# Attention and a two-layer network in one kernel: two copies put ahead of two weight sums, output transposes moved later

## The chip, the cores and the metric

The kernel runs on one core of a Trainium2 chip. Its time is the device time in microseconds (us), the median of three runs. The engines are TensorE (PE: matmuls; PEld: its weight loads, issued by the same sequencer), VectorE (DVE), ScalarE (ACT), GpSimd (POOL, which issues all loads here) and SyncE (SP, which issues all stores). Each engine works through its own list of instructions in order and waits for the others through semaphores.

## What is computed

Attention over 8 batches of 8 heads, 576 tokens each, head size 64, with 16 extra keys and values ("beacons") in front that every query sees; then a network of two layers without bias on the 4608 rows of 512 that the heads make together.

```python
k_all = np.concatenate([beacon_k, k], axis=2)
v_all = np.concatenate([beacon_v, v], axis=2)
scores = scale * np.matmul(q, k_all.transpose(0, 1, 3, 2))
causal[:, Nb:] = np.triu(np.ones((S, S), dtype=bool), k=1)
scores = np.where(causal, -1000000000.0, scores)
a = np.exp(scores - scores.max(-1, keepdims=True))
a /= a.sum(-1, keepdims=True) + 1e-09
attn = np.matmul(a, v_all)
...
x = attn.transpose(0, 2, 1, 3).reshape(B * S, H * D)
h = x @ w_in
g = np.maximum(0.01 * h, h)
return g @ w_out
```

## The kernel before

**The work's units.** Attention goes by pairs of heads: pair g = 0 to 31, four to a batch. For one pair:

- q and k are loaded by POOL (step N, load_natural), and turned on PE with the identity matrix into a PSUM tile "tp", which DVE copies to SBUF (step T, turn_natural, L177 to L184; T8.0 is q of pair 8, T8.1 its k).
- Scores are matmuls (L316) whose exponentials ACT writes (L331, L335); POOL sets the masked triangles to zero (L291). From pair 8 on this runs in "blocks" of three PSUM tiles over the pairs' columns in a row.
- Values (step v, value, L376): half 0 has 12 matmuls, half 1 has 18 (L361) into a PSUM tile "av" whose last column per row is the sum of the weights; DVE takes the reciprocal (L390) and multiplies (L391) into x_nat.
- The output's turn (x_transposes, L402 to L412): five transposes on PE (L407) from x_nat into a tile "tp", and one DVE copy into xT (L412). Here it is called x8 for pair 8, and so on.

The network goes by chunks of 512 tokens, nine in all. An "up" (moe1, L416) makes 128 hidden columns of a chunk: four matmuls of 512 columns (L427) into a PSUM tile, then the leaky ReLU on ACT into gT (L435). A "down" (moe2, L501) is eight matmuls of 256 columns (L509); the second layer is done as a 2 by 2 block product with seven products instead of eight, so it needs sums of weight blocks and of token blocks, which DVE makes: weight_sums (L447: part 0 at L453; part 1, two instructions of 128 x 2048 elements at L455 and L456; part 2 at L458) and token_sums (run at L784). Product 5 reads the result of part 0, product 6 that of L455, product 7 that of L456. Two downs share a PSUM tile, which ACT (L538, L574) or DVE (L535, L571) empties after the second.

**PSUM.** One pool, ps_one, has four banks; every tile named above but two of a block's three comes from it: tp, av, an up's and a down's acc, and the two halves of a block's first tile. When a tile is asked for, it takes a bank that an earlier tile has given up, and PE's first matmul into it waits until the engine that empties that bank is done.

**The order.** All five engines' lists are in the order in which the program states the steps (tc.manual_schedule, L906). Pairs 0 to 7 and the first chunk follow strings of steps written out by hand (L920 to L939; the letters are decoded at L863). Weight sums part 1, step t1, is in the last of them, L939, just ahead of the turns of pair 8. Then a list of events with due times takes over (L965 to L1009). The time unit is one pair; pair g's scores are due about g + 0.4. The due times of interest:

| step | due at | line |
|---|---|---|
| turn of q, k (T) of pair g | g - 1.15, g - 0.85 | L972, L973 |
| values half 0 of pair g | g + 2.25 (g + 2.05 for a batch's last pair) | L976, L977 |
| values half 1 | 0.37 later | L978 |
| output's turn, pairs 8 to 30 | 0.75 after half 0 | L980 |
| finish (a batch's last: its chunks may begin) | g + 3.5 | L985 |

The events are sorted by due time. Between two of them the loop at L997 to L1009 puts as many ups and downs as a straight line of progress asks for, some eight for one unit. The output's turn of the last pair (31) is not an event: it stands in the list for the last chunks (L1012). There, two chunks' first layer is also done with seven products (in_round).

Of the kernel before, what the change touches and what calls it, by code (L numbers as in the profile page):

```python
# [15 lines left out]
def kernel(  # L16
# [139 lines left out]
    def load_qk(g, which):  # L156
        b, hp, grp, rows = where(g)
        loaded["qk", g, which] = nc.gpsimd.dma_start(  # L158
            out=raw_of(b, grp)[which][rows],
            in_=(q, k)[which][b, 2 * hp : 2 * hp + 2].rearrange("h (p i) d -> p h i d", i=RI),  # L160
        )
# [5 lines left out]
    def load_natural(g, which):  # L167
        b, hp = divmod(g, NPAIR)
        t = natpool.tile([NR, S // NR, 2, D], BF16, name=("q_nat", "k_nat")[which])
        for par in range(2):  # L170
            nc.gpsimd.dma_start(  # L171
                out=t[:, :, par],
                in_=(q, k)[which][b, 2 * hp + par].rearrange("(t p) d -> p t d", p=NR),
            )
        nat.setdefault(g, []).append(t)

    def turn_natural(g, which):  # L177
        t = nat[g][which]
        ps = ps_one.tile([128, 1024], BF16, name="tp", tag="one")
        for n in range(S // NR):  # L180
            nc.tensor.transpose(  # L181
                ps[:, n * NR : (n + 1) * NR], t[:, n].rearrange("r h d -> r (h d)"), ident[0:NR, 0:NR]
            )
        nc.vector.tensor_copy(out=operand(g, which), in_=ps[:, 0:S])  # L184
# [22 lines left out]
    def load_v_cast(b, c):  # L207
        dst = v_bufs[b % 2]
        lo = 0
        if c == 0:  # L210
            nc.gpsimd.dma_start(
                out=dst[0:NB, 0, :, 0:D], in_=beacon_v[b].rearrange("h p d -> p h d")
            )
            lo = NB
        n = ROWS[c] - lo
        nc.gpsimd.dma_start(  # L216
            out=dst[lo : ROWS[c], c, :, 0:D],
            in_=v[b, :, OFF[c] : OFF[c] + n].rearrange("h p d -> p h d"),
        )
# [9 lines left out]
    def beacon_columns(g, copy):  # L229
        b, hp = divmod(g, NPAIR)  # L230
        copy(out=k_bufs[g % NK][:, 0:NB], in_=bkT[:, b, hp])
# [26 lines left out]
    def score(g, n):  # L258
        qT, kT = qk[g]
        if n == 0:  # L260
            probs[g] = a_bufs[g % NA]
        aT = probs[g]
        parts = SCORES[n]
        sc = ps_sc.tile([128, 2, 512], FP32, name="sc", tag="sc")
        c0 = parts[0][3]
        for c, q0, w, col in parts:
            for par in range(2):
                ps_ = slice(par * 64, par * 64 + 64)
                nc.tensor.matmul(  # L269
                    out=sc[:, par, col - c0 : col - c0 + w],  # L270
                    lhsT=kT[ps_, c * 128 : (c + 1) * 128],
                    rhs=qT[ps_, q0 : q0 + w],
                    start=True,
                    stop=True,
                    skip_group_check=True,
                )
        w = sum(p[2] for p in parts)
        nc.scalar.activation(  # L278
            out=aT[:, :, c0 : c0 + w], in_=sc[:, :, 0:w], func=AF.Exp, scale=0.125
        )  # L280
# [3 lines left out]
    def mask(g, part):  # L284
        aT = probs[g]
        for lo, n, rows in MASKS[part]:
            triangle(aT, lo, n, rows)
# [82 lines left out]
    def value_ahead(g):  # L370
        if (g, 0) not in avs:
            avs[g, 0] = ps_one.tile([128, 512], FP32, name="av", tag="one")
        value_matmuls(g, 0, avs[g, 0][:, 0:396].rearrange("p (n w) -> p n w", w=66), (0, 1))
        begun.add(g)

    def value(g, half):  # L376
        if half == 0:
            xs[g] = (
                headpool.tile([128, 5, 2, D], BF16, name="x_nat", bufs=4),
                headpool.tile([128, 10], FP32, name="rec"),  # L380
            )
        x_nat, rec = xs[g]
        t0, t1 = ((0, 3), (3, 5))[half]
        av = avs.pop((g, half), None)
        if av is None:
            av = ps_one.tile([128, 512], FP32, name="av", tag="one")
        avv = av[:, 0 : (t1 - t0) * 132].rearrange("p (n w) -> p n w", w=66)
        value_matmuls(g, half, avv, range(t0 + (2 if half == 0 and g in begun else 0), t1))
        n0, n1 = t0 * 2, t1 * 2
        nc.vector.reciprocal(out=rec[:, n0:n1], in_=avv[:, :, D])  # L390
        nc.vector.tensor_tensor(  # L391
            out=x_nat[:, t0:t1].rearrange("p t e d -> p (t e) d"),
            in0=avv[:, :, 0:D],
            in1=rec[:, n0:n1, None].to_broadcast([128, n1 - n0, D]),
            op=ALU.mult,
        )
# [396 lines left out]
    def up():  # L793
        i1, n = divmod(done1[0], NF)
        assert i1 < ready[0]
        add_late()
        fc = n if i1 == 0 else n // 2 + n % 2 * HF
        moe1(i1, fc)
        if (i1, n) == (TAIL - 1, 4 * (ROUNDS - 1) + 2):
            w_in_sums(7, 0, ROUNDS - 1, first=True)  # L800
            add_due()
        add_due()
        done1[0] += 1
        turn[0] = 1
        if i1 == 0 and n >= HF and n % SLICE == SLICE - 1:
            due.extend((i1, op) for op in token_sums(i1, n + 1 - SLICE - HF, n + 1 - HF))
        elif i1 and n % (2 * SLICE) == 2 * SLICE - 1:
            due.extend((i1, op) for op in token_sums(i1, n // 2 + 1 - SLICE, n // 2 + 1))
# [41 lines left out]
    dve, act, pool = nc.vector.tensor_copy, nc.scalar.copy, nc.gpsimd.tensor_copy  # L850
# [4 lines left out]
    def finish(g, eng=0):  # L855
        if eng < 2 and g in xs:
            x_transposes(g, (dve, act)[eng])
        ready[0] = chunks_with(g)
        if g % NPAIR == NPAIR - 1:
            turn[0] = 1  # L860
            held[0] = LEAD

    def run(steps):  # L863
        for step in steps.split():
            op, a = step[0], [int(x) for x in step[1:].split(".")] if step[1:] else []
            if op == "s":
                score(*a)
            elif op == "m":
                mask(*a)
            elif op == "v":  # L870
                value(*a)
            elif op == "e":
                value_ahead(*a)
            elif op == "x":
                finish(*a)
            elif op == "l":
                load_qk(*a)
            elif op == "V":
                load_v_cast(*a)
            elif op == "N":  # L880
                load_natural(*a)
            elif op == "T":
                turn_natural(*a)
            elif op == "q" or op == "k":
                t_q(a[0], 0 if op == "q" else 1, (dve, act)[a[1] if len(a) > 1 else 0])
            elif op == "b":
                beacon_columns(a[0], (dve, act, pool)[a[1]])
            elif op == "u":
                up()
            elif op == "d":  # L890
                down()
            elif op == "w":
                unused(*a)
            elif op == "W":
                unused_ahead(*a)
            elif op == "i":
                load_w_in(a[0])
            elif op == "o":
                load_w_out(a[0])
            elif op == "t":  # L900
                weight_sums(a[0])
            else:
                raise ValueError(step)
# [11 lines left out]
    with order:  # L915
# [20 lines left out]
        cast_beacon_k(2, B, nc.gpsimd.tensor_copy)  # L936
        run("u v5.0 u v5.1 N9.0 s7.0 s7.1 m7.0 d x5 v6.0 v6.1 t0 d s7.2 s7.3")
        beacon_transposes(2, B)
        run("m7.1 m7.2 N9.1 u b8.2 b9.2 b10.2 b11.2 x6 v7.0 v7.1 d d d N10.0 N10.1 d V2.0 V2.1 x7 t1 T8.0 T8.1")  # L939


        FIRST = 2 * NPAIR
# [23 lines left out]
        events = []  # L966
        for g in range(FIRST, NG):
            if g > FIRST + 2:
                events.append((g - 3.25, 0, run, ("N%d.0" % g,)))
                events.append((g - 2.95, 0, run, ("N%d.1" % g,)))  # L970
            if g > FIRST:
                events.append((g - 1.15, 0, run, ("T%d.0" % g,)))  # L972
                events.append((g - 0.85, 0, run, ("T%d.1" % g,)))  # L973
            if g > FIRST + 3:
                events.append((g - 2.5, 0, run, ("b%d.2" % g,)))
            at = g + (2.05 if g % NPAIR == NPAIR - 1 else 2.25)  # L976
            events.append((at, 3, value, (g, 0)))  # L977
            events.append((at + 0.37, 4, value, (g, 1)))  # L978
            if g < NG - 1:
                events.append((at + 0.75, 5, x_transposes, (g, dve)))  # L980
        for m in range((TILES + 2) // 3):
            events.append((FIRST + (0.4 if m else 0.6) + 1536 / COLS * m, 2, block, (m,)))
        ends = [FIRST]
        for g in range(FIRST, NG):
            at = g + (2.5 if g == NG - 1 else 3.5)  # L985
# [58 lines left out]
```

## Time and profile before

| | us |
|---|---|
| median of three runs | 349.16 |
| lowest, highest | 348.44, 354.82 |
| the profiled execution | 349.16 |
| its span (first to last instruction) | 347.5 |

Idle time of TensorE by stretches of the span, from the busy time of each:

| stretch, us | length | PE busy | PE idle |
|---|---|---|---|
| 0 to 25 | 25.0 | 22.91 | 2.1 |
| 25 to 52 | 27.0 | 26.68 | 0.3 |
| 52 to 61 | 9.0 | 6.88 | 2.1 |
| 61 to 270 | 209.0 | 204.80 | 4.2 |
| 270 to the end | 77.5 | 72.56 | 4.9 |

The hand-written order ends near 57 us with the turns of pair 8; from there to 280.5 us the events run; then the last chunks. The costliest groups by busy time are the ups' matmuls (L427, 119.0 us), the ACT step behind them (L435, 71.2), the masks on POOL (L291, 62.4) and the exponentials (L335, 51.7). How to read the rows: a line of the timeline gives start, duration, engine, line of the code, operation, the tile written and the tiles read, the shape, and in brackets the idle time of the engine before it and what ended that. A line of waits gives the engine and line that waited, for whom, the total in us, how often, and the longest. In the forty slices a digit is the busy share in tenths, and PEclk the granted clock in tenths of full speed.

### The profile page before, as it was taken

Reading aid. Unit: us, or ns where it says so; the run is one execution under the profiler, and the core shown is the slowest. Engines: PE = TensorE matmul, PEld = TensorE weight load, DVE = VectorE, ACT = ScalarE, POOL = GpSimd, SP = SyncE. Lnnn points to the kernel's source line nnn. Section 1 sums busy time; section 2 is a strip of 40 time slices with the busy share of each in tenths; the row PEclk is TensorE's granted clock in tenths of the full one; section 3 lists DMA queues with packets and bytes.
Section 4 is the critical chain, followed back from the end, with each engine's and each line's share of the span. In section 5 each row is a group of like instructions: output and inputs, shape, how many; then the busy total and the mean of one; then the engine's idle time right before and its main releaser. Section 6 shows DMA issues by size and latency. Waiting matters only on the chain.

```text
span 347.5 us, 9479 instructions
## 1 busy us (share of the span) xinstructions
PE 333.8 (96%) x3920; PEld 243.8 (70%) x3950; DVE 202.6 (58%) x424; ACT 206.1 (59%) x349; POOL 187.2 (54%) x354
## 2 busy tenths in 40 slices
PE   8999997999999999999999999999999999999995
PEld 5574576666678558855688888855885578688784
DVE  3472599446556255555536465735555779757854
ACT  4869860687546775457645775477546554647510
POOL 8895979997966666648755787566222000000000
PEclk9999999999999999999999999999999999999999
DMA  8999999996997996779968895889111000100113
GB/s 133 136 203 163 161 202 92 105 152 42 80 77 112 94 66 45 94 96 58 82 66 128 55 66 38 126 82 62 11 62 63 2 0 32 60 33 3 60 62 122
DMA packets 110124, 28.96 MB, mean 83 GB/s; under 512 B 96720, under 2 KB 107856, under 8 KB 110080
## 3 DMA queue, kind: packets, MB, share of 16 engines
q0 software_dynamic: 99824, 18.54, 70.9%
q1 hardware_dynamic: 9984, 9.73, 8.5%
q8 instruction: 31, 0.51, 0.6%
q14 instruction: 13, 0.11, 0.1%
q10 hardware_dynamic: 272, 0.07, 0.1%
HBM read 37.22 MB, written 9.44 MB: 134 GB/s over the span
## 4 chain that ended last, share of the span: by engine, by line
PE 83%; ACT 6%; DVE 3%; DMA 3%; POOL 2%; issue 1%; ACTq 0%; POOLq 0%
PE acc L427 28%; PE acc L509 20%; PE sc L509 11%; PE av L361 8%; PE sc L316 6%; PE acc L662 4%; ACT aT L335 3%; DMA v_aug<-in_v_dram 3%; PE tp L181 2%; PE tp L407 2%; ACT gT L435 2%; PE sc L269 1%; DVE x_nat L391 1%; POOL gsum L158 1%; ACT aT L331 1%
## 5 line engine op out<-in xcount | busy, mean ns | idle before, releaser
L427 PE MATMUL acc<-xT,w_in_sb 128*128 128x512 bf16 (+1 forms) x530 | 119.0, 354 | 2.5 <-ACT gT L435 0.7
L291 POOL TENSOR_SCALAR_AFFINE_SELECT aT<-aT 128x256 bf16<-128x256 bf16 (+2 forms) x160 | 62.4, 417 | 74.4 <-ACT aT L331 48.5
L435 ACT ACTIVATE gT<-acc 128x512 bf16<-128x512 f32 x124 | 71.2, 624 | 44.2 <-PE acc L427 43.7
L427 PEld LDWEIGHTS <-w_in_sb 128*128 128x128 bf16 x560 | 50.6, 98 | 40.3 <-issue 4.2
L509 PEld LDWEIGHTS <-gT 128*128 128x128 bf16 x576 | 54.0, 98 | 8.8 <-issue 1.8
L335 ACT ACTIVATE aT<-sc 128x1024 bf16<-128x1024 f32 (+3 forms) x64 | 51.7, 893 | 0.0
L509 PEld LDWEIGHTS <-gsum 128*128 128x128 bf16 x432 | 40.7, 98 | 7.8 <-DVE gsum L784 0.9
L390 DVE RECIPROCAL rec<-av 128x6 f32<-128x6 f32 (+1 forms) x64 | 11.9, 186 | 57.8 <-PE av L361 57.8
L331 ACT ACTIVATE aT<-sc 128x512 bf16<-128x512 f32 (+3 forms) x64 | 29.0, 520 | 27.6 <-PE sc L316 27.3
L361 PEld LDWEIGHTS <-aT 128*128 128x128 bf16 (+1 forms) x960 | 36.8, 98 | 9.9 <-issue 3.1
L361 PE MATMUL av<-v_aug,aT 128*128 128x65 bf16 (+1 forms) x960 | 39.4, 194 | 1.7 <-DMA v_aug<-in_v_dram 0.9
L216 POOL DMA_DIRECT2D v_aug<-in_v_dram x40 | 34.1, 857 | 5.0 <-DMA w_in_sb<-in_moe_w_in_dram 4.6
L509 PE MATMUL acc<-w_out_sb,gT 128*128 128x256 bf16 x288 | 36.1, 273 | 0.0
L171 POOL DMA_DIRECT2D q_nat<-in_q_dram x48 | 34.7, 728 | 0.5 <-issue 0.5
L171 POOL DMA_DIRECT2D k_nat<-in_k_dram x48 | 34.7, 729 | 0.0
L391 DVE TENSOR_TENSOR x_nat<-av,rec 128x384 bf16<-128x384 f32 (+1 forms) x64 | 31.4, 491 | 2.2
L278 ACT ACTIVATE aT<-sc 128x1024 bf16<-128x1024 f32 (+3 forms) x32 | 25.9, 875 | 2.8 <-PE sc L269 2.8
L509 PE MATMUL acc<-w_sum,gsum 128*128 128x256 bf16 x192 | 24.6, 273 | 0.0
L316 PE MATMUL sc<-qT,kT 64*128 64x80 bf16 (+22 forms) x384 | 22.0, 250 | 0.3 <-ACT gT L435 0.3
L412 DVE COPY xT<-tp 128x576 bf16<-128x576 bf16 x30 | 13.7, 456 | 13.5 <-PE tp L407 13.4
L574 ACT COPY p<-acc 128x512 f32<-128x512 f32 x15 | 9.0, 603 | 18.3 <-PE acc L509 18.3
L316 PEld LDWEIGHTS <-kT 64*128 64x128 bf16 x384 | 12.8, 94 | 9.0 <-issue 5.7
(104 smaller groups left out, 419.2 us busy)
## 6 DMA issues: line engine op xcount, KB each, us to landing
out_dram<-p SPq DMA_DIRECT2D x25, 256.0 KB, 2.3
q_nat<-in_q_dram POOLq DMA_DIRECT2D x48, 72.0 KB, 3.3
k_nat<-in_k_dram POOLq DMA_DIRECT2D x48, 72.0 KB, 3.5
v_aug<-in_v_dram POOLq DMA_DIRECT2D x24, 128.0 KB, 4.5
out_dram<-u SPq DMA_DIRECT2D x9, 256.0 KB, 2.7
w_in_sb<-in_moe_w_in_dram POOLq DMA_DIRECT2D x2, 1024.0 KB, 13.0
w_out_sb<-in_moe_w_out_dram POOLq DMA_DIRECT2D x2, 1024.0 KB, 10.3
gsum<-in_q_dram POOLq DMA_DIRECT2D x8, 144.0 KB, 6.2
```

The costliest lines, as they stand in the source:

```text
L171: nc.gpsimd.dma_start(out=t[:, :, par], in_=(q, k)[which][b, 2 * hp + par].rearrange("(t p) d -> p t d", p=NR),)
L216: nc.gpsimd.dma_start(out=dst[lo : ROWS[c], c, :, 0:D], in_=v[b, :, OFF[c] : OFF[c] + n].rearrange("h p d -> p h d"),)
L278: nc.scalar.activation(out=aT[:, :, c0 : c0 + w], in_=sc[:, :, 0:w], func=AF.Exp, scale=0.125)
L291: nc.gpsimd.affine_select(out=view, in_=view, compare_op=ALU.is_ge, fill=0.0, base=128 - n if lo == 0 else 0, channel_multiplier=-1, patte ...
L316: nc.tensor.matmul(out=(sc[par] if apart else sc[:, par])[:, at : at + b - a], lhsT=kT[ps_, c * 128 : (c + 1) * 128], rhs=qT[ps_, q0 : q0 ...
L331: nc.scalar.activation(out=probs[g][:, par, lo:hi], in_=sc[par][:, at : at + hi - lo], func=AF.Exp, scale=0.125)
L335: nc.scalar.activation(out=probs[g][:, :, lo:hi], in_=sc[:, :, at : at + hi - lo], func=AF.Exp, scale=0.125)
L361: nc.tensor.matmul(out=avv[:, n, 0 : D + 1], lhsT=aT[0 : ROWS[c], par, a0 : a0 + 128], rhs=va[0 : ROWS[c], c, 2 * hp + par, :], start=(c = ...
L391: nc.vector.tensor_tensor(out=x_nat[:, t0:t1].rearrange("p t e d -> p (t e) d"), in0=avv[:, :, 0:D], in1=rec[:, n0:n1, None].to_broadcast( ...
L427: nc.tensor.matmul(out=acc[:, lo:hi], lhsT=w_in_cols(fc, j), rhs=xT[:, j, x0 : x0 + hi - lo], start=(j == 0), stop=(j == NJ - 1), skip_gro ...
L435: nc.scalar.activation(out=gT[i][:, fc, :], in_=acc, func=AF.Prelu, alpha=0.01)
L509: nc.tensor.matmul(out=acc[:, lo : lo + HD], lhsT=left(i, n, fc, tile), rhs=right(n, fc), start=(lo == 0 and fc == 0), stop=(fc == HF - 1) ...
```

## The change

Two places. In the last hand-written string, step t1 (L455 and L456 on DVE) moves from ahead of pair 8's two turns to behind them. In the list of events, the output's turn is due 1.05 units after its values' first half instead of 0.75.

```diff
         beacon_transposes(2, B)
-        run("m7.1 m7.2 N9.1 u b8.2 b9.2 b10.2 b11.2 x6 v7.0 v7.1 d d d N10.0 N10.1 d V2.0 V2.1 x7 t1 T8.0 T8.1")
+        run("m7.1 m7.2 N9.1 u b8.2 b9.2 b10.2 b11.2 x6 v7.0 v7.1 d d d N10.0 N10.1 d V2.0 V2.1 x7 T8.0 T8.1 t1")
...
             events.append((at, 3, value, (g, 0)))
             events.append((at + 0.37, 4, value, (g, 1)))
             if g < NG - 1:
-                events.append((at + 0.75, 5, x_transposes, (g, dve)))
+                events.append((at + 1.05, 5, x_transposes, (g, dve)))
```

## The prediction

> **What bounds the kernel now.** I read the page's busy row and its forty slices first, then the chain that ended last, then what PE waited for, then the timeline at each of those waits. The page, rows 1 and 2 and the summary of the chain:
>
> ```profile
> PE 333.8 (96%) x3920; PEld 243.8 (70%) x3950; DVE 202.6 (58%) x424; ACT 206.1 (59%) x349; POOL 187.2 (54%) x354
> ...
> PE   8999997999999999999999999999999999999995
> ...
> PEclk9999999999999999999999999999999999999999
> ...
> PE 83%; ACT 6%; DVE 3%; DMA 3%; POOL 2%; issue 1%; ACTq 0%; POOLq 0%
> ```
>
> TensorE is the bound: 333.8 of 347.5 us, at full clock throughout. Only PE's idle time can be won: 347.5 - 333.8 = 13.7 us. The busy time by stretches (PE's column in windows of my choice) puts 25.0 - 22.91 = 2.1 of it before 25 us and 77.5 - 72.56 = 4.9 after 270, the change touching neither but for one stop at 270; 9.0 - 6.88 = 2.1 lie in 52 to 61 us, 209 - 204.80 = 4.2 in 61 to 270. So some 7 us is the most that a change of order here can bring. PE's waits name two rows of interest:
>
> ```profile
> PE tp L407 <- DVE x_nat L391: 1.6, 5, 0.6
> PE tp L181 <- DVE qT L184: 1.5, 1, 1.5
> ```
>
> L407 are the turns of the outputs (x_transposes), L181 those of q and k (turn_natural). The timeline from 57.4 us shows the second:
>
> ```profile
> 57.84 1.22 DVE L455 TENSOR_TENSOR w_sum<-w_out_sb,w_sum 128x2048 bf16<-128x2048 bf16 x1
> ...
> 58.09 1.04 PE L509 MATMUL acc<-w_sum,gsum 128*128 128x256 bf16 x8
> ...
> 58.97 1.22 DVE L456 TENSOR_TENSOR w_out_sb<-w_out_sb 128x2048 bf16<-128x2048 bf16 x1
> 60.10 0.45 DVE L184 COPY qT<-tp 128x576 bf16<-128x576 bf16 x1
> 60.47 0.45 DVE L184 COPY kT<-tp 128x576 bf16<-128x576 bf16 x1
> 60.61 0.41 PE L181 MATMUL tp<-ident,k_nat 96*128 96x96 bf16 x6 [1.48 <-DVE qT L184]
> ```
>
> Pair 8's q was turned at 57.26, but its copy stands behind both weight sums and ends at 60.55. Pair 9's k needs a fifth bank of a pool of four, so PE waits for that copy. The other wait, at pair 8's output:
>
> ```profile
> 78.95 0.42 PE L181 MATMUL tp<-ident,q_nat 96*128 96x96 bf16 x6
> 79.30 0.17 DVE L390 RECIPROCAL rec<-av 128x4 f32<-128x4 f32 x1
> 79.44 0.34 PE L407 MATMUL tp<-ident,x_nat 112*128 112x112 bf16 x3
> 79.50 0.42 DVE L391 TENSOR_TENSOR x_nat<-av,rec 128x256 bf16<-128x256 f32 x1
> 79.98 0.27 PE L407 MATMUL tp<-ident,x_nat 128*128 128x128 bf16 x2 [0.21 <-DVE x_nat L391]
> 80.05 0.57 PEld L427 LDWEIGHTS <-w_in_sb 128*128 128x128 bf16 x4
> 80.09 1.03 PE L427 MATMUL acc<-xT,w_in_sb 128*128 128x512 bf16 x3
> ```
>
> The turn comes before DVE has divided the values, so it stops in the middle.
>
> **The change, first edit: pair 8's turns ahead of the sums.** weight_sums issues only two DVE instructions, so PE's, ACT's, POOL's and SP's orders stay; only DVE's changes. Copies follow each other at 60.47 - 60.10 = 0.37 us. After x7's copy (57.46) come pair 8's at 57.84 and 58.21, L455 from 58.58 to 59.80, L456 from 59.71 to 60.93, pair 9's copies at 60.84 and 61.21, where they are now. PE reaches pair 9's k at 58.09 + 8 x 0.109 = 58.96 (sixteen unhindered matmuls of this form start 0.109 apart); q's bank is free at 58.29. It runs at once instead of at 60.61: 1.65 us saved.
> What could be late next: product 6 reads L455's result. PE gets there at 58.96 + 0.26 + 0.87 = 60.09, L455 ends at 59.80: 0.3 us to spare. Its bank (pair 8's k) is free at 58.66. The first score block wants two banks at 61.83; pair 9's copies end at 61.29 and 61.66. Nothing takes over, though margins are 0.2 to 0.3.
> Two rules of the Trainium skill are weighed here. The row says idle 1.48. "Perfetto Trace Analysis", section Tensor Engine Instruction, says that a matmul's end is estimated from its size, so idle behind it is only as good as that estimate; starts are observed, and give 1.65. I take 1.65; the other gives 0.17 less. The second rule speaks against the edit: "Trainium Kernel Development and Optimization", Best Practices, reads steady bubbles as PSUM running out. By that, four banks wanted by five tiles stay so in any order, and the gain is 0. But the row's releaser is a copy that sat ready for 2.3 us behind two sums of 1.13 each: the bank is freed late, not missing. I follow the row.
>
> **Second edit: output turns at +1.05 instead of +0.75 (L980).** Sorting the events and stepping the loop at L997-1009 for both offsets gives the same sequence of ups, downs, q/k turns, values and blocks; only the turns of pairs 8 to 30 (23 of them) stand two to four fills later. Eleven now follow the next pair's first half of values (x8, x9, x12, x13, x16, x17, x20, x21, x24, x25, x29), two follow that step and a k turn (x10, x22), ten stand among ups and downs. Each issues five weight loads, five matmuls and one DVE copy; no DMA, nothing on ACT, POOL or SP. Moving the work itself costs nothing: 0.26 us of PE (57.00 to 57.26 in the timeline) leave one place and enter another.
> Gained, the stops for data. A q turn and an output turn together take 0.52; from the start of the q turn to the next up I find 80.09 - 78.95 = 1.14 (x8), 87.61 - 86.52 = 1.09 (x9), 159.74 - 158.74 = 1.00 (x17), 168.86 - 167.85 = 1.01 (x18); x29 has no q turn and takes 270.67 - 269.66 = 1.01 for 0.26. Lost there: 0.62 + 0.57 + 0.48 + 0.49 + 0.75 = 2.91 us. Later by some 2.5 us, all of them find their data done.
> Gained, stops for a bank that an early turn holds: the up behind x16 waits (150.90 - 150.31 = 0.59, for ACT), and similarly behind x28 (0.49), x13 and x25 (0.41 each). With one tile less in flight the first goes; the others shrink to the next bank, by 0.3, 0.2, 0.2. Sum 1.29.
> Lost, new stops for a bank where ACT is draining exponentials. The worst two: x9 now stands between pair 10's values (PE leaves them at 91.69) and the first down of chunk 1, and takes the one free bank. The down must wait until ACT has emptied the last up but one (91.92 + 0.60 = 92.52): it ends near 93.45 instead of 92.74; less the turn's own 0.26 that is 0.45 lost. x22 does the same before a down at 209.48, whose bank comes at 210.21: 0.51. Smaller: x20 0.18, x10 0.2 (the k turn there is followed by the existing 0.71 wait for ACT's copy at 99.64), x8 0.2. Some ten ups and values keep only 0.1 to 0.3 us of slack; 0.3 for all. Sum 1.84.
> DVE itself: the copies are as many as before; behind the moved copy stand the next rec or a token sum, 0.37 later, and the ups and downs in between run 0.37 ahead in exchange. I cost that at 0, covered by DVE's 42% idle; where the cover fails (x14, x18, x26 stand within four sums of 0.6), product 6 would wait at most 0.37, 1.1 us in all. SP's stores follow the DVE adds and end in nothing PE needs. POOL is past its loads: pair 9's k landed 2.8 us before use, pair 10's 4.1, later ones over 5, so 2 to 4 us less lead is affordable.
>
> **Sum.** -1.65 - 2.91 - 1.29 + 1.84 = -4.0 us. Span 347.5 becomes 343.5; the 1.66 us around it (349.16 - 347.5) stay: **345.2 us**. The profiled execution is the median one of the three shown (348.44, 349.16, 354.82).
>
> **The rivals.**
> Half eaten: POOL is busy without a break from 51 to 81 us, and the chain holds ACT's exponentials for 3%. If PE, running ahead, meets POOL or ACT, the first edit's 1.65 comes back as waits before 90 us and 2.4 us remain: 346.8. Against it: no PE wait for POOL exists in the trace, and ACT stood idle 1.2 to 1.8 us before each block there.
> Nothing moves, because the allocation of banks falls out differently and each saved stop reappears at the next tile: 349.2. For it: ups after a block do run at ACT's pace. Against: behind all five data stops ACT idles 1.38 us or more, so it isn't what sets the pace there.
> Slower: bank shortage at the new places. Eleven turns now sit right behind values, where their bank is held through rec and division (0.2 + 0.56) plus the copy. If the x9 stop of about 0.5 us repeats, the 5.85 gained are used up at 12 places; at all 23 it is 11.5 - 5.85 = +5.6: 354.8. With half the turns worse than that, it passes 2%. For it: one bank too few already costs PE 0.6 to 0.7 at 99 and 151 us. Against: at most new places the bank wanted is free 0.4 us or more beforehand.
> The short description speaks of transposing transfers; the diff removes none, and the kernel has none. It changes two positions and nothing else.
>
> **How the numbers follow.** Likeliest case 0.57 (own range 343.2 to 346.6), half eaten 0.20 (346.6 to 348.8), nothing 0.07 (about 349.2), slower 0.16 (349.5 to 355). Lower end: all gains at full size, 1.65 + 2.91 + 1.9, no loss, is 342.7; I stop at 343.0. The upper end reaches past "nothing" into the mild slower cases, 350.0; outside are about 0.05 below and 0.13 above. The bound of 2% is 7 us, about what a measurement of this kernel can tell from no change: below 342.2 I put 0.03 (more than every stop counted above), above 356.1 0.03, between them 0.94.
>
> **What would show it.** Pair 9's k turn (L181) near 59.0 with no wait, pair 8's copies ahead of L455, and all later stages about 1.6 us earlier. The row of L407 waiting for x_nat gone from PE's waits. New waits of a down (L509) for ACT's gT near 90 us and for DVE near 206. Wrong if: L407's waits go but PE's idle sum stays near 13.7; if DVE makes PE wait for gsum; if PE waits for a DMA before 70 us.

## The result, and the profile after

| us | before | after |
|---|---|---|
| median | 348.89 | 345.32 |
| lowest, highest (4 runs each) | 348.44, 354.82 | 344.77, 351.31 |
| ratio | | 0.9896, interval 0.9873 to 0.9920 |
| span of the profiled execution | 347.5 | 343.8 |

The time falls by 3.6 us (by the interval 2.8 to 4.4): about 1%, within 2% of no change, as forecast (345.2). Now and then an execution of either kernel takes some 350 to 355 us; the ratios leave those out.

The page of the kernel after, its busy row and TensorE's forty slices:

```profile
PE 333.0 (97%) x3920; PEld 244.1 (71%) x3950; DVE 201.6 (59%) x424; ACT 205.9 (60%) x349; POOL 186.7 (54%) x354
...
PE   8999999999999999999999999999999999999995
```

The dent in the seventh slice (a 7 before) is gone. PE is still the bound. The stretch 52 to 61 us (length, then busy time of PE, PEld, DVE, ACT and POOL, granted clock, DMA share, GB/s):

```profile
52.00:61.00 9.00, 8.36 (x108) 7.40 (x105) 8.23 (x16) 1.26 (x3) 9.00 (x17) 1.00 1.07 91
```

PE's column was 6.88: it gains 1.48 us there. The timeline of after at this place:

```profile
57.73 0.45 DVE L184 COPY qT<-tp 128x576 bf16<-128x576 bf16 x1
...
58.10 0.45 DVE L184 COPY kT<-tp 128x576 bf16<-128x576 bf16 x1
...
58.46 1.22 DVE L455 TENSOR_TENSOR w_sum<-w_out_sb,w_sum 128x2048 bf16<-128x2048 bf16 x1
...
58.86 0.42 PE L181 MATMUL tp<-ident,k_nat 96*128 96x96 bf16 x6
...
59.12 2.79 PE L509 MATMUL acc<-w_sum,gsum 128*128 128x256 bf16 x24
59.59 1.22 DVE L456 TENSOR_TENSOR w_out_sb<-w_out_sb 128x2048 bf16<-128x2048 bf16 x1
```

Pair 8's two copies stand ahead of the sums; pair 9's k is turned at 58.86 with no wait in brackets, and 24 matmuls of the products follow without a break: L455 ends at 59.68, 0.3 us before product 6 wants it. PE's waits in after, some of the rows:

```profile
PE tp L407 <- ACT p L574: 0.7, 1, 0.7
...
PE acc L509 <- ACT p L574: 0.5, 1, 0.5
PE acc L509 <- ACT gT L435: 0.5, 1, 0.5
...
PE acc L427 <- DVE p L571: 0.2, 1, 0.2
```

Both rows of before that named a DVE tile for L407 and L181 are gone. The first row is an old stop in a new place: before, the values of pair 11 waited for the same copy (0.7), now x10 does. The two rows of 0.5 are new, and so is the last: the up behind x28 now waits for DVE's add out of a bank of two downs (L571, 260.01 to 260.69; the up starts at 260.75), where before it waited for ACT. Of the two rows of 0.5, the first in time is that of the down behind x9, in the timeline of after:

```profile
88.87 0.42 PE L407 MATMUL tp<-ident,x_nat 112*128 112x112 bf16 x5
...
89.10 1.13 ACT L435 ACTIVATE gT<-acc 128x512 bf16<-128x512 f32 x2
...
89.80 1.03 PE L509 MATMUL acc<-w_out_sb,gT 128*128 128x256 bf16 x8 [0.51 <-ACT gT L435]
```

The turn takes the one free bank; the down behind it stops until ACT has emptied an up. By starts the stop is 89.80 - 88.87 - 0.26 = 0.67 us (0.68 before rounding), 0.26 being what lies between the start of an output's turn and the start of the next step where nothing stops PE. The second, behind x22, waits for ACT's copy out of the bank of two downs:

```profile
205.63 0.42 PE L407 MATMUL tp<-ident,x_nat 112*128 112x112 bf16 x5
...
205.88 0.65 ACT L574 COPY p<-acc 128x512 f32<-128x512 f32 x1
...
206.57 1.03 PE L509 MATMUL acc<-w_sum,gT 128*128 128x256 bf16 x8 [0.52 <-ACT p L574]
```

Again 206.57 - 205.63 - 0.26 = 0.68.

### The profile page after: what moved, and what is told of

Same layout as the page of the kernel before. It is cut to its first block, busy times and chain, and to the rows that moved or that the text cites. A ratio compares the mean times of both kernels' runs of the same rounds, so it can differ in the third digit from the quotient of the medians.

```text
span 343.8 us, 9479 instructions
## 1 busy us (share of the span) xinstructions
PE 333.0 (97%) x3920; PEld 244.1 (71%) x3950; DVE 201.6 (59%) x424; ACT 205.9 (60%) x349; POOL 186.7 (54%) x354
## 4 chain that ended last, share of the span: by engine, by line
PE 82%; ACT 7%; POOL 3%; DMA 3%; issue 2%; DVE 2%; ACTq 0%; POOLq 0%
PE acc L427 28%; PE acc L509 19%; PE sc L509 11%; PE av L361 7%; PE sc L316 6%; PE acc L662 4%; ACT aT L335 4%; PE tp L181 3%; DMA v_aug<-in_v_dram 3%; PE tp L407 2%; ACT gT L435 2%; POOL gsum L158 1%; PE sc L269 1%; ACT aT L331 1%; POOL v_aug L216 1%
## 5 line engine op out<-in xcount | busy, mean ns | idle before, releaser
L361 PEld LDWEIGHTS <-aT 128*128 128x128 bf16 (+1 forms) x960 | 37.1, 98 | 8.9 <-issue 0.9
L361 PE MATMUL av<-v_aug,aT 128*128 128x65 bf16 (+1 forms) x960 | 40.0, 194 | 0.5 <-DMA v_aug<-in_v_dram 0.2
L509 PE MATMUL acc<-w_sum,gsum 128*128 128x256 bf16 x192 | 23.9, 273 | 0.0
L574 ACT COPY p<-acc 128x512 f32<-128x512 f32 x15 | 9.1, 604 | 20.7 <-PE acc L509 20.7
L184 DVE COPY qT<-tp 128x576 bf16<-128x576 bf16 x24 | 10.8, 452 | 13.0 <-PE tp L181 13.0
```

Source lines behind the costliest of these rows:

```text
L361: nc.tensor.matmul(out=avv[:, n, 0 : D + 1], lhsT=aT[0 : ROWS[c], par, a0 : a0 + 128], rhs=va[0 : ROWS[c], c, 2 * hp + par, :], start=(c = ...
L509: nc.tensor.matmul(out=acc[:, lo : lo + HD], lhsT=left(i, n, fc, tile), rhs=right(n, fc), start=(lo == 0 and fc == 0), stop=(fc == HF - 1) ...
```

## The experiments

**The theories.** A stop is what a matmul's start is late beyond its undisturbed spacing from the one before; a data stop waits for an operand, a bank stop for PSUM. A: each edit removes the stops it was seen to remove, the two are independent, and the second pays part of its gain back in new stops for a bank. B: four banks are too few, so a stop can only be displaced (no gain from order). C: what helps is that all output turns run later, not the five that stopped.

**The measure.** The load stage ahead of the change differs from one execution to the next: pair 8's q is first turned anywhere from 56.42 to 58.19 us of the span in nine of the ten profiled executions (62.93 in the tenth), more spread than an edit is worth. So besides span and ratio I compare the time from that turn's first matmul to the end of the span. For the kernel after, profiled twice, it is 286.60 and 286.63 us; for E6, also twice, 284.87 and 284.86.

| kernel | median, us | ratio to before | interval | span | first turn of pair 8 at | from there to the end |
|---|---|---|---|---|---|---|
| before | 348.89 | | | 347.5 | 57.26 | 290.19 |
| after | 345.32 | 0.9896 | 0.9873 to 0.9920 | 343.8 | 57.16 | 286.60 |
| E1, first edit alone | 348.01 | 0.9963 | 0.9947 to 0.9978 | 346.3 | 57.73 | 288.58 |
| E2, second edit alone | 346.77 | 0.9931 | 0.9910 to 0.9951 | 344.9 | 56.67 | 288.21 |
| E3, sums between q and k | 346.23 | 0.9900 | 0.9874 to 0.9926 | 344.1 | 56.67 | 287.47 |
| E4, five turns only | 345.42 | 0.9879 | 0.9856 to 0.9903 | 344.7 | 58.19 | 286.51 |
| E5, five turns out of the banks' way | 344.84 | 0.9868 | 0.9837 to 0.9899 | 348.3 | 62.93 | 285.36 |
| E6, turns at +1.40 | 343.47 | 0.9831 | 0.9806 to 0.9855 | 341.6 | 56.68 | 284.87 |
| E7, after again | 345.88 | 0.9890 | 0.9868 to 0.9913 | 343.1 | 56.42 | 286.63 |
| E8, E6 again | 344.04 | 0.9843 | 0.9813 to 0.9873 | 342.5 | 57.67 | 284.86 |

The ratios are to runs of before on the same chip: 348.93 beside E1, E2, E5 and E6, 349.58 beside E3, E4, E7 and E8.

**E1: the first edit alone.** Against before:

```diff
-... V2.0 V2.1 x7 t1 T8.0 T8.1")
+... V2.0 V2.1 x7 T8.0 T8.1 t1")
```

> Only pair 8's turns go ahead of the weight sums; output turns stay at +0.75. Theory (PE waited for a copy that stood behind two sums): PE's wait of L181 for L184 (1.48 us) is gone, pair 9's k is turned near 59.0, everything behind comes 1.65 us earlier to the end, span 345.8 to 346.0, time 0.995 of before; L407's row of waiting for x_nat stays (1.6, 5 times). Rival 1 (PSUM simply ran out): PE waits as long at the next tile, span 347.5. Rival 2 (POOL sets the pace up to 81 us): the gain comes back as waits of PE for POOL, DMA or masks before 90 us, span 347 or more.

Measured: from pair 8's turn to the end 290.19 - 288.58 = 1.61 us less; by the ratio 1.3 us (0.8 to 1.8). The L181 wait is gone, and the five data stops are what they were, in PE's waits of E1:

```profile
PE tp L407 <- DVE x_nat L391: 1.6, 5, 0.6
```

The span, 346.3, is above the expected 345.8 to 346.0, but pair 8 also came 0.47 us later than in before (57.73 against 57.26). What follows: the whole stop is won and nothing later takes it back. Theory B doesn't hold here, since the tiles and banks are as many as before.

**E2: the second edit alone.** Against before:

```diff
-                events.append((at + 0.75, 5, x_transposes, (g, dve)))
+                events.append((at + 1.05, 5, x_transposes, (g, dve)))
```

> Only the output turns go to +1.05; the weight sums stay ahead of pair 8's turns. Theory (the two edits are independent, this one is worth 3.7 - 1.65): span 345.4, time 0.994 of before; the wait of L181 (1.48 us) stays, L407 doesn't wait for x_nat, new waits of a down behind x9 and x22 (0.6 to 0.7 each). Rival (the edits share one gain, since a later turn after an earlier start meets ACT): span 344 or 346.5.

Measured: 290.19 - 288.21 = 1.98 us less; by the ratio 2.4 (1.7 to 3.1). The span, 344.9, is below the expected 345.4, and pair 8 came 0.59 us earlier than in before (56.67 against 57.26). The stop at pair 9's k stays, the five data stops go, and both new stops for a bank are there, in PE's waits of E2:

```profile
PE tp L181 <- DVE qT L184: 1.5, 1, 1.5
...
PE tp L407 <- ACT p L574: 0.7, 1, 0.7
...
PE acc L509 <- ACT p L574: 0.5, 1, 0.5
PE acc L509 <- ACT gT L435: 0.5, 1, 0.5
```

What follows: 1.61 + 1.98 = 3.59, and both together give 290.19 - 286.60 = 3.59. The edits are independent.

**E3: the sums between pair 8's q and k.** Against after:

```diff
-... V2.0 V2.1 x7 T8.0 T8.1 t1")
+... V2.0 V2.1 x7 T8.0 t1 T8.1")
```

> Pair 8's q turned ahead of the two weight sums, its k behind them; output turns at +1.05. Theory 'the bank came late': q's bank is free early, so PE's wait at pair 9's k stays gone; but pair 8's k is now copied only behind both sums, and the next that wants that bank, the first down of product 6 (or what follows it), waits instead, some 0.7 to 1.5 us. Span 344.5 to 345.3, 0.7 to 1.5 above the changed kernel's 343.8; PE's busy time in 52 to 61 us below the changed kernel's 8.36 by as much. Rival 'four banks are too few for five tiles': the stop at pair 9's k returns at about 1.5 and the span is about 345.4. Rival 'the saved stop came from something else': nothing changes, 343.8.

Measured: 287.47 - 286.60 = 0.87 us more than after (medians 346.23 and 345.88, intervals overlap; the trace decides). The span, 344.1, is below the expected 344.5 to 345.3, since pair 8 came 0.49 us earlier than in after. PE's busy time in 52 to 61 us is 7.65 against 8.36. Timeline of E3:

```profile
57.24 0.45 DVE L184 COPY qT<-tp 128x576 bf16<-128x576 bf16 x1
...
57.60 1.22 DVE L455 TENSOR_TENSOR w_sum<-w_out_sb,w_sum 128x2048 bf16<-128x2048 bf16 x1
...
58.37 0.42 PE L181 MATMUL tp<-ident,k_nat 96*128 96x96 bf16 x6
...
58.74 1.22 DVE L456 TENSOR_TENSOR w_out_sb<-w_out_sb 128x2048 bf16<-128x2048 bf16 x1
...
59.87 0.45 DVE L184 COPY kT<-tp 128x576 bf16<-128x576 bf16 x1
...
60.38 1.91 PE L509 MATMUL acc<-w_sum,gsum 128*128 128x256 bf16 x16 [0.71 <-DVE kT L184]
```

The q copy is in front, so pair 9's k is turned unhindered at 58.37. The k copy now stands behind both sums, and the first matmuls of product 6 stop for it instead. What follows: the stop goes where the copy behind the sums goes, and its size is that copy's lateness. A bank that is short whatever the order would have kept the stop at pair 9's k.

**E4: only the five turns that stopped.** Against after:

```diff
-                events.append((at + 1.05, 5, x_transposes, (g, dve)))
+                events.append((at + (1.05 if g in (8, 9, 17, 18, 29) else 0.75), 5, x_transposes, (g, dve)))
```

> First edit whole; of the 23 output turns only the five that stopped for their data (pairs 8, 9, 17, 18, 29) at +1.05, the rest back at +0.75. Theory 'the gain of the second edit is these stops': the five stops stay gone; the waits for a bank return at pair 16's up (0.59), pair 28's (0.49) and grow at pairs 13 and 25 (0.41); the new stops behind x22 (0.68) and x20 (0.20) vanish, the one behind x9 (0.68) stays. Summed over PE's starts 16.9 - 1.65 - 2.86 + 0.68 + 0.24 = 13.3 against the changed kernel's 13.2: span 343.7 to 344.3. Rival 'running later as a whole is what helps' (one tile less in flight everywhere): most of the gain goes with the other 18, span 345.2 to 345.6.

Measured: 286.51, that is 0.1 less than after; the medians 345.42 and 345.88 don't part. Its span of 344.7 is longer than after's only because pair 8 came a microsecond later (58.19 against 57.16); by the span alone this run would have been misread. The old stop behind x16 is back, and with it the row of ups in PE's waits of E4:

```profile
PE acc L427 <- ACT gT L435: 0.7, 2, 0.4
```

The timeline of E4 at pair 16 shows it, 149.86 - 149.01 - 0.26 = 0.59 us:

```profile
149.01 0.42 PE L181 MATMUL tp<-ident,k_nat 96*128 96x96 bf16 x6
...
149.86 1.02 PE L427 MATMUL acc<-xT,w_in_sb 128*128 128x512 bf16 x4 [0.43 <-ACT gT L435]
```

Those behind x28 (0.49) and near x13 and x25 (0.41 each) are back too, while the ones behind x22 (0.68) and x20 (0.20) are gone. What follows: the five moves carry all of the second edit's gain. The other eighteen win stops for banks and lose as many. Theory C falls.

**E5: the five turns with a new stop behind them put further on.** Against after:

```diff
-                events.append((at + 1.05, 5, x_transposes, (g, dve)))
+                late_by = {8: 1.4, 9: 1.4, 20: 1.4, 22: 1.2, 28: 1.2}.get(g, 1.05)
+                events.append((at + late_by, 5, x_transposes, (g, dve)))
```

> Both edits, and five turns still later: x8, x9, x20 at +1.40 (behind both halves of the next pair's values), x22 and x28 at +1.20. Theory (what the changed kernel lost, it lost because these turns took the one free bank while ACT was draining): the waits behind x9 (0.68) and x22 (0.68) go, those of 0.2 to 0.36 behind x8, x20 and x28 shrink; span 343.8 - 1.7 = 342.1 (341.7 to 342.7). Rival (PE only meets ACT a little later, so the waits move to the next tile): span 343.5 to 344.

Measured: 285.36, 1.24 us less than after. The span of its profiled execution says nothing, since TensorE was granted 0.66 of its clock in the first 25 us; windows of E5:

```profile
0.00:25.00 25.00, 22.78 (x262) 12.22 (x262) 8.32 (x26) 13.73 (x17) 18.62 (x39) 0.66 1.53 151
```

Only 262 matmuls fell into that stretch instead of the 416 of after; in the stretches from 25 to 270 us the granted clock is 1.00, behind them 0.99, as in after. The stops behind x8, x9, x20, x22 and x28 are gone (0.24, 0.68, 0.20, 0.68, 0.36 in after, 2.16 together). In their place stand 0.38 at a block of scores near x28, 0.18 at the q turn that now follows x8, and 0.17 inside the down near x9, which before had too. What follows: the new stops were a matter of place, with the tiles and banks as many as before, and most of what they cost can be had back.

**E6 and E8: all turns at +1.40.** Pair 30 stays at +1.05. Against after:

```diff
-                events.append((at + 1.05, 5, x_transposes, (g, dve)))
+                events.append((at + (1.40 if g < 30 else 1.05), 5, x_transposes, (g, dve)))
```

> Both edits, all output turns at +1.40 (x30 at +1.05). Nearly every turn now follows the second half of the next pair's values. Theory (places matter through the bank alone, and at these places one is free): like the run with five turns moved, span 341.7 to 342.7, only the wait of 0.7 to 0.9 us for ACT's copy p at pair 11's values left. Rival (later is worse: the copies stand behind more DVE work and tiles are held longer, or an up waits for xT): span above 343.8, with PE waiting for DVE.

> Both edits, but all output turns of pairs 8 to 29 at +1.40 (pair 30 stays at +1.05). If the new stops for a bank are only a matter of place, the gain seen for this repeats beside the changed kernel on one chip: 1.5 to 2.2 us less, 343.0 to 343.7. If it was one lucky execution of the load stage: within 0.5 of the changed kernel.

> The changed kernel itself, on the chip of the other three runs, as the measure for them: 345.2 us, span 343.8 give or take 0.6, since the load stage before 52 us differs by that much from one execution to the next.

Measured: 284.87 and 284.86, 1.74 us less than after; medians 343.47 and 344.04, beside after's 345.88 on the chip of E8. E7 came out at 345.88 where 345.2 was expected, with before 0.7 higher there too; its ratio, 0.9890, is close to the first one's, 0.9896. E8's gain of 345.88 - 344.04 = 1.8 is inside the expected 1.5 to 2.2, its time 0.3 above the expected 343.7, on a chip where before is 0.7 slower. E6's span, 341.6, is 0.1 below its range. What PE's waits of E6 still list behind pair 8's turn, both of which before had too:

```profile
PE av L361 <- ACT p L574: 0.7, 1, 0.7
...
PE sc L316 <- ACT gT L435: 0.3, 1, 0.3
```

and pair 9 in the timeline of E6:

```profile
89.38 0.72 PE L361 MATMUL av<-v_aug,aT 128*128 128x65 bf16 x18
89.93 0.42 PE L407 MATMUL tp<-ident,x_nat 112*128 112x112 bf16 x5
90.19 1.04 PE L509 MATMUL acc<-w_out_sb,gT 128*128 128x256 bf16 x8
```

The turn now follows the second half of the values, and the down behind it starts 0.26 later, with no stop. What follows: this is the best version run, 1.6 to 1.7% under before. PE's matmuls other than the output turns run in the same order in E4, E7 and E8, so nothing but the turns' places differs there. E6 gets there by the same five data stops, without the stops for a bank that +1.05 makes.

## Why the prediction was right

The forecast was -4.0 us and 345.2; measured are -3.57 by medians, -3.59 from pair 8's turn to the end, and 345.32. The median came as near as that partly by luck: before ran 0.27 faster this time (348.89 against 349.16), and from there -4.0 would have given 344.9, 0.4 under the measured time. Step by step, by the starts of PE's matmuls in the traces of before and after (the first row from E1):

| term | forecast | measured |
|---|---|---|
| first edit, stop at pair 9's k | -1.65 | -1.61 (E1) |
| five data stops | -2.91 | -2.86 |
| bank stops freed (x16, x28, x13, x25) | -1.29 | -1.18 |
| new bank stops at x9, x22, x20, x10, x8 | +1.54 | +1.63 |
| small ones | +0.3 | about +0.5 |
| sum | -4.0 | -3.5; from turn to end -3.59, 0.1 not assigned |

- **First edit.** Right with its places: L455 ended 0.3 us before product 6 wanted it, as worked out, and nothing behind it stopped. The Trainium skill ("Perfetto Trace Analysis", section Tensor Engine Instruction) says that a matmul's end is estimated and not measured; in keeping with it, the starts (1.65) were a better measure than the idle time in brackets (1.48): E1 gives 1.61. The other rule weighed, that consistent bubbles can mean that PSUM ran out ("Trainium Kernel Development and Optimization", Best Practices), was taken to make the gain 0: E1 and E3 show that here the bank came late.
- **Data stops.** Right one by one (0.61, 0.56, 0.48, 0.48, 0.73). E4 shows that these five alone carry the edit.
- **Freed bank stops.** x16's 0.59 went whole, x13's and x25's fell from 0.41 to 0.18. Only x28 was mis-sized: 0.49 fell to 0.36, not by 0.3. The next bank there is the one that DVE empties at 260.69, with an add that waited its turn in DVE's list: DVE is busy from 258.07 on, no down runs between 258.3 and 260.01, and there the add begins.
- **New bank stops.** The places were right. Behind x9 the stop is 0.68, from which 0.17 comes off that the neighbouring down had waited before: 0.51 against 0.45 forecast. x22 costs 0.68, not 0.51; x20 0.20; x8 0.24. x10 costs nothing: the 0.87 wait that pair 11's values had already is now taken by x10 itself. The page was to show ACT's gT near 90 us, which it does, and DVE near 206, which was wrong: it is ACT's copy (L574).
- **The small ones**, put at 0.3 for some ten places, are the term that failed by most. Slips below 0.17 each add up to 0.43 more than before, and two existing stops grow from 0.21 to 0.24. Half of the 0.43 stands where blocks of scores meet their neighbours, the rest where a turn meets an up or values. Which of the 23 moves makes which slip was not taken apart; E4, without the eighteen, has 0.35 less of it.
- **DVE at 0.** Right for the sums: PE's one wait for a token sum (gsum, 0.6) lies ahead of pair 8 and is the same in both. Not quite for the adds: the wait for DVE behind x28 (0.2 in the row, 0.36 by starts) is one that the forecast did not name.
- **The rivals.** "Half eaten by POOL or ACT": PE's waits from 57 to 290 us list none for POOL, and E1 keeps its 1.61. "Nothing moves": excluded by the interval. "Slower by bank shortage": its mechanism is there at x9 and x22 at 0.68 each, beyond the 0.5 it was priced at, but at two places and not at twelve; x20 and x8 cost 0.2 each.

## What to carry to other kernels

Before you add a buffer, look at the queue of the engine that frees it: a bank whose copy is ready but stands behind other work on an in-order engine comes late, and changing two places in that queue gave back the whole stop (1.61 us). No run here had a fifth bank, so what a buffer more would have given is open. When a step is moved to let its data come ready, see what the next step needs in the place it moves to: moving five of the 23 turns gave the whole gain, and the places at +1.05 gave back 1.7 us, most of it ahead of tiles whose bank was still being emptied, that places a few steps further on kept. Differences of less than a microsecond are compared from a fixed instruction behind the load stage to the end; there two executions of one kernel agree within 0.03 us, where their spans differ by 0.7 to 0.9.

## What was not expected of the hardware

Two executions of one program differ here almost only in their load stage. After's two have spans of 343.8 and 343.1, E6's two 341.6 and 342.5, while behind pair 8's turn they are equal to 0.03 and 0.01 us. What differs are PE's waits for loads: E8 waited 0.9 for q (tile gsum, L245) and 0.9 for v (L361), E6, the same kernel, 0.8 for q and not at all for v, and came to pair 8 0.99 us earlier (56.68 against 57.67). In PE's waits of E8:

```profile
PE tp L245 <- DMA gsum<-in_q_dram: 0.9, 1, 0.9
PE av L361 <- DMA v_aug<-in_v_dram: 0.9, 1, 0.9
```

What makes one load of the same program land later than in the next execution stays open; no run here was made for it.
